# Scalings of the coarse probabilities on ScalarE, one more unit with exps by tiles, and a seventh unit in the first stage of an attention and feed-forward kernel

## The chip, the core and the metric

The kernel runs on one core of a Trainium2 chip. The metric is the device time of that core in microseconds (us), the median of several executions. The engines are called PE (TensorE), DVE (VectorE), ACT (ScalarE), POOL (GpSimd) and SP (SyncE, which issues the DMAs here). PEld is PE's load of the stationary operand.

## What is computed

```python
# q, k, v: (4, 8, 576, 64)
def sm_attn(qq, kk, vv):
    s = scale * np.matmul(qq, kk.transpose(0, 1, 3, 2))
    ...
    return np.matmul(a, vv)          # a = softmax(s)
q_d = q.reshape(B, H, Sd, 4, D).mean(axis=3)     # k_d, v_d the same; Sd = 144
out_up = np.repeat(sm_attn(q_d, k_d, v_d), 4, axis=2)
mask = np.abs(pos[:, None] - pos[None, :]) < 4
scores = np.where(mask, scale * q k^T, -1e9)
out_local = softmax(scores) @ v
x = (out_up + out_local) as (2304, 512)          # rows: batch and position, columns: head and dim
h = x @ w_in                                     # (2304, 2048)
out = (h * np.tanh(log1p(np.exp(np.minimum(h, 20.0))))) @ w_out
```

So there is a coarse attention over positions averaged by fours, a local attention over a band of 7 positions, and a feed-forward part over the sum of both.

## The kernel before

**Units.** Attention is cut into 16 units, one for each batch b (0 to 3) and each pair of heads p (0 to 3). Counted in order, unit 4b+p is (b, p). A unit runs in `attention()` (line 332): the load of `qk` (L350) and sums by fours on DVE (L351, `qkd`); the coarse scores `sc` on PE (L366), their maximum on DVE (L369, L371), three exps with sums on ACT (L373, `A`), the reciprocal (L376, L378), and the scaling of the probabilities. The scaling has two forms: for the units in the list `AMUL` three activations of 128x128 on ACT (L381), for the others one DVE instruction over 128x384 (L384). A small rest, `Ar`, is scaled by DVE in either form (L387). The local scores `sl` (L400, L405) are exponentiated in one of two forms too. For the units in `AEXP` that is nine activations with their own sums, one for each tile of 38 columns (L415, each followed by a read of the accumulator), after a maximum and a small product on DVE (L411, L413). For the others it is a maximum and a subtraction on DVE (L422, L423), one exp over 128x342 on ACT (L425) and a sum on DVE (L426). DVE then scales `L` (L428 to L430). `vv` is loaded (L435) and POOL makes the averaged values (L438, L440, `vd`). PE transposes (L449, L450, L477, L483), ACT copies out of PSUM, PE makes the products with the values (L464, L468, L492), and DVE and ACT add both parts and split them into two words, written into the tiles `x` (L505, L517, L519).

**Slots.** The feed-forward part is 96 slots in `slot()` (line 566): chunk c (0 to 5) of 384 rows against block f (0 to 15) of 128 hidden columns. A slot has twelve matmuls into `h` (L579), five ACT and three DVE instructions (L593 to L605, ending in `g`) and nine matmuls into three accumulators `acc` (L618). Chunks 0 and 1 are interleaved in slots 0 to 31; then come chunks 2 to 5, sixteen slots each. The weights of block f are loaded by SP (L549) into three staging buffers in turn and rebuilt from 64-bit words by ACT and DVE in `load_w()` (L551 to L561).

**Order.** Every operation is recorded with an engine, a planned duration, the buffers it reads and writes, and a priority (lower goes first). `Plan.order()` (line 147) then lays out the order of every engine beforehand: at each step an engine that is free takes the ready operation of lowest priority. The chip executes each engine's list strictly in that order, SP's too. The priorities are: of unit (b, p), `ATT[b][0] + ATT[b][1]*p + UNIT[(b, p)]`, with `VOFF` added for its load of `vv`; of the weights of block f, `WPRI[0] + WPRI[1]*f`, with `WPRI[2]` more for `wo` and `WDMA` more for the load itself; of a slot's `h` about its number s, of its elementwise chain s + 0.2, of its `acc` s + LAG - 0.5, with one LAG for slots under 20, one for 20 to 59 and one from 60.

**Stages.** The first `NPRO` units belong to the first stage (line 661 on). They take turns on four sets of SBUF buffers, `att0`, `att1`, `att2`, `att`, and may use seven PSUM buffers (`props` 4, `attps` 3). The units behind them use the set `att` and the three buffers of `attps` alone, each buffer in the order of the units. When every operation of the first stage is planned to be done (`gate`, line 672, and `done`, line 697), `props` and the sets `att0` to `att2` are closed, and the PSUM of the slots and the weight buffers of blocks 5 to 15 open. The accumulators of chunk 1 lie in `attps` (line 610), so that units 8 and later cannot use it before slot 31 has ended. While PE has nothing to do in the plan, matmuls of constants are put in (`warm`, L705).

Of the kernel before, what the change touches and what calls it, by code (L numbers as in the profile page):

```python
# [19 lines left out]
P = 128  # L20
BIG = 1e30
CH = 384
LAG = (3.0, 4.0, 4.0)
FA = 5
SETS = 3
ATT = {0: (-900, 20), 1: (-46, 10.0), 2: (-4, 16.5), 3: (46, 4.0)}
WPRI = (9.565474018610834, 2.2, 7.7)
UNIT = {(0, 0): -1, (0, 1): -3, (0, 2): -2, (0, 3): -3, (1, 0): 7, (1, 1): -1, (1, 3): 1, (2, 0): 1, (2, 1): -1, (2, 2): 5, (2, 3): 1, (3, 0): 2, (3, 1): 2, (3, 2): 1, (3, 3): -2, (1, 2): -7}
WARM = True
NPRO = 6  # L30
STICK = 15
VOFF = 20
WDMA = 6
PIPE0 = (1, 0, 1)
PIPE1 = (1, 0, 1)
LEAD = 1
PMASK = (0, 1)
AMUL = ((0, 2), (1, 0), (1, 2))
AEXP = ((0, 1), (0, 3))
NMISH = (3, 2)  # L40
TAIL = 0
TICK, BUSY, PACE = 3413.3, 3060, 1.6
# [36 lines left out]
class Plan:  # L79
# [6 lines left out]
    def buf(self, group, tag, shape, dtype=F32, bufs=1, name=None):  # L86
        return Buf(self, group, tag, shape, dtype, bufs, name or f"{tag}_{len(self.ops)}")

    def op(self, eng, dur, fn, r=(), w=(), prio=None, after=(), cold=None, cols=0, gap=0):
        o = Op()  # L90
        o.eng, o.dur, o.fn, o.cold, o.cols, o.gap = eng, dur, fn, cold or 2 * dur, cols, gap
        o.prio = self.prio if prio is None else prio
        o.deps, o.bufs, o.outs, o.seq, o.raw, o.hold = set(after), [], [], len(self.ops), set(), 0.0
        for items, writes in ((r, False), (w, True)):
            for x in items:
                b, key = x if isinstance(x, tuple) else (x, None)
                write = writes or b.group.endswith("ps")
                if b not in o.bufs:
                    o.bufs.append(b)
                    b.left += 1  # L100
                for k, (wr, rd) in b.marks.items():
                    if key is None or k is None or k == key:
                        o.deps.update(wr)
                        o.raw.update(wr)
                        if write:
                            o.deps.update(rd)
                if write:
                    if key is None:
                        b.marks = {None: ({o}, set())}
                    else:  # L110
                        b.marks[key] = ({o}, set())
                else:
                    b.marks.setdefault(key, (set(), set()))[1].add(o)
        o.deps.discard(o)
        self.ops.append(o)
        return o
# [154 lines left out]
def dve(n, fast=False):  # L271
    return 69 + (0.52 if fast else 1.042) * n


def act(n, psum=False, extra=0):
    return (52 if psum else 94) + 0.833 * n + 93 * extra
# [6 lines left out]
class Kernel:  # L283
# [48 lines left out]
    def attention(self, b, p, sb, ps, padded, loose):  # L332
# [45 lines left out]
        op("dve", 88, lambda: nc.vector.reciprocal(cst()[:, 3], cst()[:, 2]), w=[cst])  # L378
        if (b, p) in AMUL:
            for m in range(3):  # L380
# [28 lines left out]
        wide = lambda i: lst()[:, i, :, None].broadcast_to([P, T, KW])  # L409
        if (b, p) in AEXP:  # L410
            op("dve", dve(T * KW), lambda: nc.vector.tensor_reduce(out=lst()[:, 0], in_=sl3(), op=ALU.max, axis=AX.X),  # L411
# [20 lines left out]

        pv_ = pl.prio + VOFF
        vv, vd = buf("vv", [P, 18, P]), buf("vd", [P, 2, P])
# [99 lines left out]
    def load_w(self, f):  # L534
# [6 lines left out]
        for nm, src in (("wi", wi), ("wo", wo)):  # L541
            pl.prio = prio + (WPRI[2] if nm == "wo" else 0)
            st_ = pl.buf("stg", "stg", [P, 512, 2], I32, self.nstg, f"stg_{nm}{f}")
# [5 lines left out]
            op("sp", P * 4096 / RATE, lambda st_=st_, src=src: nc.sync.dma_start(  # L549
                st_().rearrange("p (c f) w -> p c (f w)", c=4), src), w=[st_], prio=pl.prio + WDMA)  # L550
            op("act", act(512), lambda hf=hf: nc.scalar.activation(hf(), hf(), AF.Copy, scale=2.0 ** -112), w=[h])  # L551
# [14 lines left out]
    def slot(self, s, c, f):  # L566
# [46 lines left out]
        for i in range(3):  # L613
# [7 lines left out]
            gi = [g] if len(parts) == 1 else [(g, 2 * i), (g, 2 * i + 1)]  # L621
            op("pe", 700, mm2, r=[*gi, wo], w=[a_], cols=1536, prio=s + LAG[(s >= 20) + (s >= 60)] - 0.5 + 0.1 * i)
            if not last:
# [11 lines left out]
    def run(self, ctx):  # L635
# [28 lines left out]
        for b in (0, 1):  # L664
            for p in range(self.NPAIR):
                if len(units) == NPRO:
                    break
                units.append((ATT[b][0] + ATT[b][1] * p + UNIT.get((b, p), 0), self.attention(
                    b, p, sets[len(units) % len(sets)], ("props", "attps"),
# [4 lines left out]
        for f in range(self.NF):  # L674
            pl.prio = WPRI[0] + WPRI[1] * f
            self.load_w(f)
# [11 lines left out]
        def units(bs):  # L688
            us = [(ATT[b][0] + ATT[b][1] * p + UNIT.get((b, p), 0), self.attention(b, p, "att", "attps", probs["att"], False))
                  for b in bs for p in range(self.NPAIR) if 4 * b + p >= NPRO]  # L690
            self.record(us, PIPE1)
# [82 lines left out]
```

## Time and profile before

| | us |
|---|---|
| median of 3 runs | 522.82 |
| lowest and highest | 521.39, 525.77 |
| the profiled execution, its own time | 524.82 |
| its span, first to last instruction | 522.7 |
| mean granted TensorE clock, share of full | 0.997 |

The profile is of one execution. Busy time counts an engine from the start to the end of its instructions; successive instructions overlap a little, so the step from one start to the next is shorter than a duration. Rows of a timeline give the start, the time, the engine, the line, what is written from what, a count, and in brackets the idle time ahead and what ended it.

### The profile page before, as it was taken

To read this page: it belongs to the slowest core of one execution; us is meant where nothing else is said; L and a number is where in the kernel's file an instruction comes from. 1 tells how busy PE (TensorE), PEld (TensorE's weight loads), DVE (VectorE), ACT (ScalarE), POOL (GpSimd) and SP (SyncE) were. 2 spreads that over 40 slices of the span, in tenths; PEclk is the share of its full clock that TensorE was granted. 3 is DMA by queue.
4 is the path that set the end of the run, shared out by engine and by line. 5 is a ranking of instruction groups with operands and counts; after the bars stand their busy time and mean duration, and the time that the engine had idled before them with its cause. 6 is when DMAs were issued, how large, how long until landed. Compare 5 with 4: busy or idle time off the path is not lost.

```text
span 522.7 us, 11854 instructions
## 1 busy us (share of the span) xinstructions
PE 504.2 (96%) x4896; PEld 435.1 (83%) x4896; DVE 322.6 (62%) x703; ACT 358.0 (68%) x866; POOL 40.4 (8%) x62
## 2 busy tenths in 40 slices
PE   7879979999999999999999999999999999999997
PEld 4657767899988999888898888889999999999995
DVE  6869989999999633677852885564333333333332
ACT  3668778899898756667666666665666556666663
POOL 6431011000000000010110110110000000000000
PEclk9998999999999999999999999999999999999999
DMA  8774465544544001333300453020001000010001
GB/s 345 294 270 150 141 201 201 162 161 130 193 129 154 1 0 57 112 139 136 126 16 0 139 198 131 9 93 0 1 16 46 0 1 1 0 62 0 1 0 60
DMA packets 11861, 50.66 MB, mean 97 GB/s; under 512 B 1312, under 2 KB 1312, under 8 KB 9760
## 3 DMA queue, kind: packets, MB, share of 16 engines
q1 hardware_dynamic: 11808, 49.91, 26.9%
q8 instruction: 38, 0.62, 0.5%
q14 instruction: 15, 0.12, 0.1%
HBM read 45.19 MB, written 4.72 MB: 95 GB/s over the span
## 4 chain that ended last, share of the span: by engine, by line
PE 59%; DVE 14%; ACT 3%; issue 1%; DVEq 0%
PE acc L618 27%; PE h L579 27%; DVE g L605 1%; PE pve L492 1%; DVE mA L594 1%; DVE stg_wo L554 1%; DVE stg_wi L554 1%; PE pt L477 1%; DVE stg_wi L557 1%; DVE x L505 1%; PE pvo L492 1%; DVE x L519 1%; DVE wi L561 1%; DVE Ar_att L387 1%; DVE stg_wo L557 1%
## 5 line engine op out<-in xcount | busy, mean ns | idle before, releaser
L579 PE MATMUL h<-x,wi 128*128 128x384 f32 x1152 | 220.5, 338 | 1.0 <-DVE mH L600 0.9
L618 PE MATMUL acc<-wo,g 128*128 128x512 f32 x864 | 217.8, 395 | 0.3 <-ACT g L603 0.3
L579 PEld LDWEIGHTS h<-x,wi 128*128 128x128 f32 x1152 | 203.3, 188 | 10.3 <-DVE mH L600 2.7
L618 PEld LDWEIGHTS acc<-wo,g 128*128 128x128 f32 x864 | 159.7, 188 | 30.0 <-ACT g L603 0.8
L605 DVE SCALAR_TENSOR_TENSOR g<-mH,g 128x384 fp32r<-128x384 f32 (+1 forms) x98 | 53.5, 547 | 92.9 <-ACT g L603 92.8
L593 ACT ACTIVATE mA<-h 128x384 f32<-128x384 f32 (+1 forms) x98 | 46.8, 480 | 58.6 <-PE h L579 58.1
L596 ACT ACTIVATE mA<-mA 128x384 f32<-128x384 f32 (+1 forms) x98 | 50.5, 517 | 39.7 <-DVE mA L594 39.0
L594 DVE TENSOR_SCALAR mA<-mA 128x384 f32<-128x384 f32 (+1 forms) x98 | 38.7, 396 | 52.7 <-ACT mA L593 52.7
L600 DVE SCALAR_TENSOR_TENSOR mH<-mA,h 128x384 f32<-128x384 f32 (+1 forms) x98 | 52.7, 539 | 18.9 <-ACT mA L599 18.8
L597 ACT ACTIVATE mA<-mA,one 128x384 f32<-128x384 f32 (+1 forms) x98 | 59.5, 608 | 2.4
L603 ACT ACTIVATE g<-mH 128x384 fp32r<-128x384 f32 (+1 forms) x98 | 50.0, 512 | 4.5 <-PE acc L618 2.6
L599 ACT ACTIVATE mA<-mA 128x384 f32<-128x384 f32 (+1 forms) x98 | 49.7, 508 | 0.8
L438 POOL TENSOR_TENSOR vv<-vv 128x512 f32<-128x512 f32 x16 | 21.7, 1358 | 303.5 <-DMA vv<-in_vv_dram 285.1
L373 ACT ACTIVATE A<-sc,cst 128x144 f32<-128x144 f32 x48 | 17.8, 375 | 15.3 <-DVE cst L371 9.2
L517 ACT ACTIVATE x<-x 128x384 fp32r<-128x384 f32 (+1 forms) x32 | 12.4, 434 | 19.8 <-DVE x L505 19.7
L351 DVE TENSOR_REDUCE qkd<-qk 128x288 f32<-128x1152 f32 x16 | 21.5, 1346 | 5.7 <-DMA qk<-in_qk_dram 5.7
L492 PEld LDWEIGHTS pve<-PT,vv 38*64 38x64 f32 x640 | 20.4, 134 | 4.7 <-ACT PT L484 2.6
L492 PE MATMUL pve<-PT,vv 38*64 38x32 f32 x640 | 22.5, 220 | 0.0
L492 PE MATMUL pvo<-PT,vv 38*64 38x32 f32 x512 | 18.3, 221 | 1.8 <-issue 1.6
L705 PE MATMUL warm<-ident 128*128 128x512 bf16 x61 | 17.3, 408 | 1.6 <-POOL ident masks.py:199 1.6
L492 PEld LDWEIGHTS pvo<-PT,vv 38*64 38x64 f32 x512 | 16.4, 133 | 2.0 <-issue 1.7
L366 PE MATMUL sc<-qkd 64*64 64x144 f32 x192 | 16.7, 300 | 0.1
(82 smaller groups left out, 445.1 us busy)
## 6 DMA issues: line engine op xcount, KB each, us to landing
vv<-in_vv_dram SPq DMA_DIRECT2D x16, 1152.0 KB, 6.0
qk<-in_qk_dram SPq DMA_DIRECT2D x16, 582.0 KB, 5.9
stg_wi<-in_w_in_dram SPq DMA_DIRECT2D x16, 512.0 KB, 3.5
stg_wo<-in_w_out_dram SPq DMA_DIRECT2D x16, 512.0 KB, 3.9
out_dram<-o SPq DMA_DIRECT2D x18, 256.0 KB, 2.1
```

Source lines behind the costliest of these rows:

```text
L438: op("pool", gps(512), lambda: nc.gpsimd.tensor_tensor(out=vc()[:, :, 0:2], in0=vc()[:, :, 0:2], in1=vc()[:, :, 2:4], op=ALU.add), w=[(vv, ...
L492: nc.tensor.matmul(o_()[64 * h:64 * h + 64, c0:c0 + 32], vw()[64 * e:64 * e + KW, t // 2, f, 64 * h:64 * h + 64], PT()[64 * e:64 * e + KW, ...
L579: nc.tensor.matmul(h()[:, :CH], w()[:, a, kt * P:(kt + 1) * P], x()[:, b_, :], start=kt == 0 and j == 0, stop=kt == 3 and j == 2)
L593: op("act", act(n, True), lambda o_=o_: nc.scalar.activation(A()[:, o_], h()[:, o_], AF.Exp), r=[h_], w=[a_])
L594: op("dve", dve(n, True), lambda o_=o_: nc.vector.tensor_scalar(A()[:, o_], A()[:, o_], float(math.exp(20.0)), 1.0, op0=ALU.min, op1=ALU.a ...
L596: op("act", act(n), lambda o_=o_: nc.scalar.activation(A()[:, o_], A()[:, o_], AF.Square), w=[a_])
L597: op("act", act(n, False, 1), lambda o_=o_: nc.scalar.activation(A()[:, o_], A()[:, o_], AF.Ln, bias=self.one), w=[a_])
L599: op("act", act(n), lambda o_=o_: nc.scalar.activation(A()[:, o_], A()[:, o_], AF.Exp, scale=-1.0), w=[a_])
L600: op("dve", dve(n), lambda o_=o_: nc.vector.scalar_tensor_tensor(out=H()[:, o_], in0=A()[:, o_], scalar=0.5, in1=h()[:, o_], op0=ALU.subtr ...
L603: op("act", act(n), lambda o_=o_: nc.scalar.activation(g()[:, 0, o_], H()[:, o_], AF.Copy, scale=-2.0), r=[x_], w=[one])
L605: op("dve", dve(n), lambda o_=o_: nc.vector.scalar_tensor_tensor(out=g()[:, 1, o_], in0=H()[:, o_], scalar=-2.0, in1=g()[:, 0, o_].bitcast ...
L618: nc.tensor.matmul(a_(), g()[:, a, i * P:(i + 1) * P], wo()[:, b_], start=first and j == 0, stop=last and j == 2)
```

## The change

Only constants change; the functions stay as they are.

- `AMUL` has all eight units of b = 0 and 1 in place of (0, 2), (1, 0), (1, 2): five more units scale on ACT by three instructions (L381) and not on DVE by one (L384).
- `AEXP` has (1, 1) as well: its local exps go by nine tiles (L411 to L415) and not by L422 to L426.
- `NPRO` is 7 in place of 6: unit 6, (1, 2), joins the first stage. It uses the set `att2` and all seven PSUM buffers, and the gate waits for it. Unit 7, (1, 3), is then the only one behind it on `att` until unit 8.
- Priorities: `VOFF` 40 in place of 20 and `WDMA` 10 in place of 6 (loads of `vv` and of weights later), the step of the weights 2.58 in place of 2.2, LAG 3.5 and 6.0 in place of 3.0 and 4.0 for slots under 20 and from 20 to 59, and new places of the units: (0, 0) at -903, was -901; (1, 0) at -36, was -39; b = 2 at about -4.6, 7.0, 26.6, 36.2, was -3, 11.5, 34, 46.5; b = 3 at about -10.6, 1.7, 19.0, 31.3, was 48, 52, 55, 56.

```diff
-LAG = (3.0, 4.0, 4.0)
+LAG = (3.5, 6.0, 4.0)
-ATT = {0: (-900, 20), 1: (-46, 10.0), 2: (-4, 16.5), 3: (46, 4.0)}
-WPRI = (9.565474018610834, 2.2, 7.7)
-UNIT = {(0, 0): -1, (0, 1): -3, (0, 2): -2, (0, 3): -3, (1, 0): 7, (1, 1): -1, (1, 3): 1, (2, 0): 1, (2, 1): -1, (2, 2): 5, (2, 3): 1, (3, 0): 2, (3, 1): 2, (3, 2): 1, (3, 3): -2, (1, 2): -7}
+ATT = {0: (-900, 20), 1: (-46, 10.0), 2: (-5.642684844573687, 13.604260058964448), 3: (-12.599534886270362, 15.294421654670417)}
+WPRI = (9.565474018610834, 2.5796502663643848, 7.7)
+UNIT = {(0, 0): -3, (0, 1): -3, (0, 2): -2, (0, 3): -3, (1, 0): 10, (1, 1): -1, (1, 3): 1, (2, 0): 1, (2, 1): -1, (2, 2): 5, (2, 3): 1, (3, 0): 2, (3, 1): -1, (3, 2): 1, (3, 3): -2, (1, 2): -7}
-NPRO = 6
+NPRO = 7
-VOFF = 20
-WDMA = 6
+VOFF = 40
+WDMA = 10
-AMUL = ((0, 2), (1, 0), (1, 2))
-AEXP = ((0, 1), (0, 3))
+AMUL = ((0, 0), (0, 1), (0, 2), (0, 3), (1, 0), (1, 1), (1, 2), (1, 3))
+AEXP = ((0, 1), (0, 3), (1, 1))
```

## Rows read from the trace of the kernel before

**Rows 1.** The page's first line.
```profile
span 522.7 us, 11854 instructions
```

**Rows 2.** Busy time by stretch: the stretch, its length, then for PE, PEld, DVE, ACT and POOL the busy us and the number of instructions, the granted clock as a share of full speed, the DMA share and GB/s.
```profile
0.00:31.00 31.00, 25.99 (x566) 15.88 (x566) 22.49 (x54) 16.75 (x73) 14.92 (x38) 1.00 0.79 308
31.00:71.00 40.00, 36.27 (x866) 27.95 (x866) 35.62 (x91) 29.67 (x108) 5.96 (x6) 0.96 0.54 194
71.00:102.88 31.88, 29.10 (x214) 24.52 (x215) 28.41 (x55) 25.54 (x53) 4.62 (x4) 1.00 0.53 179
102.88:211.04 108.16, 107.47 (x539) 96.94 (x538) 81.93 (x164) 88.79 (x175) 0.00 (x0) 1.00 0.31 100
211.04:353.69 142.65, 140.22 (x1889) 120.92 (x1889) 97.03 (x216) 94.27 (x252) 14.92 (x14) 1.00 0.28 100
```

**Rows 3.** The chain of work that ended last, in order of time: start, us, what. Two pieces of one slot, and the last piece of the chain.
```profile
357.85 2.10 PE h L579 x12
359.95 2.08 PE acc L618 x9
...
510.68 8.22 PE acc L618 x36
```

**Rows 4.** Busy time of line 579 alone (the `h` matmuls) in one stretch: PE, PEld, clock, DMA.
```profile
211.04:353.69 142.65, 55.91 (x289) 50.43 (x289) 1.00 0.28 100
```

**Rows 5.** Timeline of PE around unit 8, the first of the units that run between slots (its L492 matmuls left out).
```profile
215.16 0.95 PE L366 MATMUL sc<-qkd 64*64 64x144 f32 x12
...
216.82 2.35 PE L579 MATMUL h<-x,wi 128*128 128x384 f32 x12
...
221.09 0.49 PE L449 MATMUL at<-ident,A 128*128 128x128 f32 x3
...
221.44 2.35 PE L579 MATMUL h<-x,wi 128*128 128x384 f32 x12
223.72 0.47 PE L464 MATMUL pvo<-AT,vd 128*64 128x144 f32 x4
...
224.91 1.63 PE L618 MATMUL acc<-wo,g 128*128 128x512 f32 x6
```

**Rows 6.** Timeline of PE in the first 103 us: the first of a unit's L492 matmuls and what follows them, the first `h` of all, the first product with `vd` of unit 7, and the `h` of the ninth slot (slot 8).
```profile
43.77 0.25 PE L492 MATMUL pve<-PT,vv 38*64 38x32 f32 x2
...
45.05 0.66 PE L477 MATMUL pt<-ident,L_att 128*128 128x128 f32 x4
...
61.70 1.32 PE L579 MATMUL h<-x,wi 128*128 128x384 f32 x6
...
73.17 0.47 PE L464 MATMUL pvo<-AT,vd 128*64 128x144 f32 x4 [2.21 <-POOL vd L440]
...
102.88 2.27 PE L579 MATMUL h<-x,wi 128*128 128x384 f32 x12
```

**Rows 7.** Timeline of DVE in the first 80 us: scalings of `A` in units 1 and 5 with what follows them, the small product of unit 3's exps by tiles, and three waits; the row at 63.75 ends unit 6.
```profile
13.20 1.37 DVE L384 TENSOR_TENSOR A<-A,cst 128x384 f32<-128x384 f32 x1
14.50 0.73 DVE L387 TENSOR_TENSOR Ar_att<-A,cst 128x48 f32<-128x48 f32 x1
...
28.18 0.17 DVE L413 TENSOR_SCALAR lst<-lst 128x9 f32<-128x9 f32 x1
...
47.53 0.55 DVE L384 TENSOR_TENSOR A<-A,cst 128x384 f32<-128x384 f32 x1
48.00 0.17 DVE L428 TENSOR_SCALAR lst<-lst 128x9 f32<-128x9 f32 x1
...
52.79 0.49 DVE L505 TENSOR_TENSOR x<-pve,xd 128x320 f32<-128x320 f32 x1 [0.76 <-ACT A L381]
...
63.75 0.82 DVE L519 TENSOR_TENSOR x<-x,x 128x192 fp32r<-128x192 f32 x2
...
72.29 1.35 DVE L351 TENSOR_REDUCE qkd<-qk 128x288 f32<-128x1152 f32 x1 [1.10 <-DMA qk<-in_qk_dram]
...
75.86 0.43 DVE L552 TENSOR_SCALAR tmp_wi<-stg_wi 128x512 int32<-128x512 int32 x1 [0.88 <-ACT stg_wi L551]
```

**Rows 8.** Timeline of ACT in the first 46 us: one exp by tiles of unit 1 with its accumulator read and the next instruction; the three scalings of unit 2 and the next; the one exp of a unit that is not done by tiles and the next.
```profile
16.07 0.29 ACT L415 ACTIVATE L_att<-sl,lst 128x38 f32<-128x38 f32 x1
...
16.34 0.22 ACT L456 ACTIVATE R_att<-at 16x96 f32<-16x96 f32 x1
...
28.05 0.97 ACT L381 ACTIVATE A<-A,cst 128x128 f32<-128x128 f32 x3
28.93 0.36 ACT L373 ACTIVATE A<-sc,cst 128x144 f32<-128x144 f32 x1
...
44.92 0.48 ACT L425 ACTIVATE L_att<-L_att 128x342 f32<-128x342 f32 x1
45.30 0.37 ACT L373 ACTIVATE A<-sc,cst 128x144 f32<-128x144 f32 x1
```

**Rows 9.** Timeline of SP's queue: the issue of `vv` of unit 6, of `qk` of unit 7, and of `vv` of unit 7.
```profile
45.21 0.33 SPq L435 DMA_DIRECT2D vv<-in_vv_dram  x1
48.89 0.33 SPq L350 DMA_DIRECT2D qk<-in_qk_dram  x1
...
61.87 0.36 SPq L435 DMA_DIRECT2D vv<-in_vv_dram  x1
```

**Rows 10.** Timeline of POOL: the first sum of unit 1's values.
```profile
12.89 1.27 POOL L438 TENSOR_TENSOR vv<-vv 128x512 f32<-128x512 f32 x1 [2.00 <-DMA vv<-in_vv_dram]
```

## The prediction, made before the changed kernel was run

> **What bounds the kernel now.** I read the busy time by stretch first, then the chain of work that ended last, then the timelines of the first 103 us engine by engine. The span is 522.7 us [rows 1], 2.1 us under this execution's own 524.82.
>
> The chain shows the steady state: a slot is 2.10 us of `h` and 2.08 us of `acc` on PE, 4.18 us together, with nothing between [rows 3]. From 102.88 us, the start of slot 8 [rows 6], to 211.04 lie 26 slots; 26 x 4.18 = 108.7, and the stretch took 108.2 [rows 2]. So there PE sets the pace and nothing can be won. The same holds for the last stretch, from 353.69 to the end.
>
> In the stretch 211.04 to 353.69 PE does 24 slots (289 `h` matmuls, twelve a slot [rows 4]) and the eight units of b = 2 and 3. The slots are worth 24 x 4.18 = 100.3 us, so the units cost 142.65 - 100.3 = 42.3 us. A unit's work on PE, by steps from start to start, is 1.66 for both scores, 0.35 for the transposes of `A`, 1.19 for the products with `vd` and the transposes of `L` [rows 5] and 1.28 for L492 [rows 6]: 4.5 us, 36 us for eight. **At most 6.3 us of this stretch is loss.**
>
> Before 102.88 us PE has eight units (36 us), eight `h` and six `acc` (29.3 us): 65 of 103 us. The rest is start-up, constants and waiting. Here PE follows the others. DVE is busy 22.5 of the first 31 us, 35.6 of the next 40 and 28.4 of the 31.9 behind; ACT 16.8, 29.7 and 25.5 [rows 2]. **From 31 to 103 us DVE is the engine nearest to its limit, at 89%**, ACT is at 74 and 80%. What shortens this part moves the whole stream of slots forward, one for one.
>
> **The change part by part.** *Scalings on ACT.* Five units lose L384. Undisturbed it takes 0.47 us of DVE from start to start (47.53 to 48.00), in unit 1 it took 1.30 [rows 7]. Each gains three activations on ACT, 28.05 to 28.93, 0.88 us [rows 8]. *Exps by tiles of (1, 1).* DVE loses L423 and L426, 342 columns each; by the ratio to L384's 384 columns 0.42 us each, and gains L413, 0.17 at most [rows 7]: about 0.7 saved. ACT gains nine exps at 0.27 (16.07 to 16.34) and loses one of 0.38 (44.92 to 45.30): 2.05 us [rows 8].
>
> Units 0, 1 and 3 lie in the first 31 us, units 5 and 7 behind. So behind 31 us DVE saves 2 x 0.47 + 0.7 = 1.6 us, and ACT takes on 2 x 0.88 + 2.05 = 3.8. In 31 to 71 us that would make DVE 34.0 and ACT 33.5 of 40: level. I count the 1.6 as won, between 0 (ACT becomes the pace) and 1.6. In the first 31 us DVE saves 0.47 + 1.30 + 0.47 = 2.2 and ACT takes on 2.6. DVE has 8.5 us idle there and ACT 14.2, so I take 0 from there; it is covered by that idle time. Without that cover the ends are a gain of 2.2 and a loss of 2.6.
>
> L384 of unit 1 took 1.37 us while POOL's L438 ran from 12.89 to 14.16 [rows 7, 10]. The Trainium skill, SBUF — State Buffer, Who interferes with whom, says that a DVE instruction with two inputs in SBUF contends with a GpSimd instruction that reads SBUF, and that ScalarE waits for nobody. The trace agrees; by that rule the moved scaling would also win back the 0.8 us of this stretch, unless the next DVE instruction with two inputs meets L438 in its place.
>
> *The seventh unit.* Unit 6 had begun long before the first `h`: its `vv` was issued at 45.21 and it ended at 64.6, the first `h` being at 61.70 [rows 6, 7, 9]. What is new is its place. On `att` it followed unit 3, and unit 7 followed it: unit 7's `qk` went out at 48.89 and its `vv` only at 61.87, once unit 6 had freed the tile [rows 9]. That is why PE waited 2.21 us for `vd` at 73.17 [rows 6]. On `att2` unit 6 follows unit 2, and unit 7 follows unit 3, whose tiles are free by 45 us. Everything behind a late load in an in-order queue moves with it: in SP's queue the weights stood behind these two loads; in DVE's queue the reduction of unit 8's `qk` at 72.29 stood 1.10 us (it needs unit 7's tile) with slot 0's last instruction and the weights behind it, and 0.88 us was lost at 75.86 for a weight whose load was late [rows 7]. Of these 1.98 us, with 0.76 us at 52.79 that was queued behind a unit-6 instruction, I count **2.2 us** as won, between 0 and 2.7. The lower place of `vv` (VOFF 40) puts `qk` of the next unit ahead of it, the lower place of weights (WDMA 10) the loads of the last units ahead of those. Both cost nothing while the loads come before their use; POOL's two sums of unit 7 follow the earlier load. With that cover gone, a late `vd` costs what it cost at 73.17, 2.2 us.
>
> *The gate* now waits for unit 6. If unit 6 ended at 64.6 as before, the first `h` would be 2.9 us later. I take 0: until then DVE has unit 7 and the weights of the first five blocks, which need no gate, and the early `h` of slots 0 and 1 were not what was late; the elementwise chain behind them was, on DVE. The bound is 2.9.
>
> *The second half.* LAG 6 lets PE take `h` further ahead of `acc`, so that a late `g` stops it less; units of b = 3 are no longer held back to slots 48 on. Both act on the 6.3 us of loss and on nothing else. No row shows a run with another LAG. I take a quarter, 1.6 us: most of the loss is inside the units' own chains on a single set of buffers, which stays single. The ends are 5 won, and 4 lost if units packed closer hold up the slots' chain on ACT and DVE. LAG 3.5 and the step of the weights only shift what DVE does first among work that must all be done by 103 us: 0.
>
> **Sum:** -1.6 - 2.2 - 1.6 = **-5.4 us**. Against this execution's own time that is 524.82 - 5.4 = 519.4; the execution is 2.0 above the median, so against the median 522.82 it is **517.4 us**, faster by 1.03%.
>
> **Rivals.** *(a) Hidden.* The start of slot 8 is set by the total of DVE's and ACT's work for units, weights and slots, and the waits that go are filled by waits elsewhere, since ACT gains 3.8 us where it is already at 74%. For it: ACT and DVE come out level. Against it: the waits at 72 to 76 us have one cause, the shared set, and it goes. Then only the second half counts: 522.8 - 1.6, about 521. That the seventh unit changes nothing, because it was already running at 45 us, is this case too.
>
> *(b) ScalarE becomes the bound.* All 6.4 us of new ACT work (5 x 0.88 + 2.05) lands on the path of the first stage: in the first 31 us unit 1 has its nine exps already and gets its scaling as well, and from 31 to 71 us ACT goes from 29.7 to 33.5 of 40. It decides once ACT's idle time there cannot be used because each idle piece is a wait for PE or DVE in the chain of one unit. Then 522.8 + 6.4 = **529**, slower. Against it: in 31 to 71 us 10.3 us of ACT are free and several units are in flight. The Trainium skill, ScalarE: Activation LUTs, Rules for kernel authors, puts multiplications on VectorE rather than ScalarE, and so speaks for this rival; the rows agree about the price, 0.88 against 0.47 us a unit, but not about which engine has room.
>
> *(c) All waits go.* The start gains 1.6 + 2.7 + 2.2, the second half 5: 522.8 - 11.5 = 511.3.
>
> **Chances.** The forecast (513.5 to 520.5) 0.46; hidden 0.24; ScalarE 0.13; all waits go 0.17. About 1% (5.2 us, so 517.6 and 528.0) is what a measurement of this kernel can tell from no change. Faster by over 1%: 0.17 and 0.28 of the forecast's 0.46, together 0.45. Within 1%: 0.18 and 0.24, together 0.42. Slower: 0.13. A range from 511.5 to 525.5 leaves out (b) and less than half of (c), under 2 in 10.
>
> **What would show it.** Right: `vv` of unit 7 is issued well before 61.87, PE does not wait for `vd` near 73, slot 8's `h` starts about 99 us (102.88 less 3.8) and stretch 211 to 354 is about 1.6 us shorter for its 24 slots and eight units. DVE's busy time falls by about 4 us and ACT's grows by about 6.4. Wrong: slot 8 at 103 us or later with ACT above 90% from 31 to 71 us is (b); an unchanged start with the waits gone elsewhere is (a); a first `h` later than 64 us with DVE idle ahead of it means that the gate costs what I took as nothing.

## The result, and the profile after

The changed kernel takes **529.96 us** (528.68 to 533.33, 4 runs) against 522.91 before: ratio **1.0121**, 95% interval 1.0081 to 1.0161. Timed again beside the kernel before (run e5) it is 527.54 against 523.52, 1.0069 (1.0041 to 1.0096). It is slower where I had forecast faster by 1%. The ratios leave out the executions marked as slow on record (one of 988 us, the profiled one of e8, one of 822 us in e13, one of 528.7 us in e9 and four of the kernel before); the medians count all.

The profiled execution took 533.33 us, the longest of the first four. Its busy time by stretch answers to [rows 2]; the columns are the same.

```profile
0.00:31.00 31.00, 26.57 (x576) 16.35 (x576) 20.64 (x51) 20.13 (x89) 14.41 (x38) 1.00 0.89 347
31.00:71.00 40.00, 34.78 (x797) 24.51 (x798) 30.88 (x75) 26.86 (x112) 8.18 (x8) 0.81 0.38 146
71.00:102.88 31.88, 31.34 (x248) 26.55 (x247) 29.12 (x57) 27.05 (x55) 2.42 (x2) 0.97 0.49 170
102.88:211.04 108.16, 108.00 (x546) 97.42 (x545) 85.12 (x170) 90.34 (x179) 0.00 (x0) 1.00 0.31 103
211.04:353.69 142.65, 136.93 (x1868) 116.83 (x1867) 97.94 (x216) 93.48 (x248) 15.37 (x14) 1.00 0.30 106
```

Two things differ. From 31 to 71 us the granted clock is 0.81 (before 0.96), and DVE and ACT are *less* busy than before, 30.9 and 26.9 us. ACT waits for PE there (10.5 us, of them 8.6 for the transposes of `A`, L450); DVE waits 2.9 us for PE and 5.6 for ACT. From 211 to 354 us PE is busy 3.3 us less than before: it stands more.

PE's timeline shows the first, with the rows that answer to [rows 6].

```profile
9.42 2.12 PE L705 MATMUL warm<-ident 128*128 128x512 bf16 x9
...
59.73 0.31 PE L492 MATMUL pve<-PT,vv 38*64 38x32 f32 x1 [1.35 <-issue]
...
69.02 4.05 PE L705 MATMUL warm<-ident 128*128 128x512 bf16 x9
...
73.56 0.77 PE L579 MATMUL h<-x,wi 128*128 128x384 f32 x3
74.25 0.47 PE L464 MATMUL pvo<-AT,vd 128*64 128x144 f32 x4
...
106.89 1.40 PE L579 MATMUL h<-x,wi 128*128 128x384 f32 x7
```

PE stood 1.35 us, from 58.38 to 59.73, for nothing that the profile shows. Towards the end of this stand the clock fell to half (1.2 GHz): its share is 1.00 from 58 to 59 us, 0.77 in the next microsecond and 0.50 in the one after. Nine constants then took 4.05 us where nine took 2.12 at full clock. The first `h` came at 73.56 (before 61.70), slot 8 at 106.89 (before 102.88). But the wait for `vd` of [rows 6] is gone at 74.25. SP's queue shows why; the rows are the issue of unit 8's `qk`, of the first weights and of unit 7's `vv`, which left at 61.87 before [rows 9].

```profile
49.35 0.33 SPq L350 DMA_DIRECT2D qk<-in_qk_dram  x1
49.73 0.43 SPq L549 DMA_DIRECT2D stg_wi<-in_w_in_dram  x1
50.25 0.38 SPq L435 DMA_DIRECT2D vv<-in_vv_dram  x1
```

From the start of slot 8 to the end of the span it takes 531.3 - 106.9 = **424.4 us**; before it was 522.7 - 102.9 = **419.8**. So of 8.6 us in the profiled executions 4.0 arise ahead of slot 8 and **4.6 behind it**. PE's waits from 103 to 360 us (total us, times, longest), first before, then now, are these:

```profile
PE at L450 <- DVE Ar_att L387: 2.1, 4, 0.7
PE h L579 <- DVE mH L600: 0.7, 2, 0.5
PE pvo L464 <- ACT AT L453: 0.3, 1, 0.3
```

```profile
PE pvo L468 <- ACT R_att L456: 2.7, 3, 1.2
PE h L579 <- DVE mH L600: 2.1, 3, 1.1
PE sl L405 <- issue: 0.6, 1, 0.6
PE pve L492 <- ACT PT L484: 0.4, 1, 0.4
```

They sum to 3.1 us before and 5.8 now. Of the 4.6 us these waits show 2.7, and the wait of `h` for L600 is 1.4 of the growth; the rest of the 4.6 is in no wait listed here.

### The profile page after: what moved, and what is told of

It is laid out like the page before. It is cut to its first block, busy times and chain, and to the rows that moved or that the text cites. A ratio compares the mean times of both kernels' runs of the same rounds, so it can differ in the third digit from the quotient of the medians.

```text
span 531.3 us, 11838 instructions
## 1 busy us (share of the span) xinstructions
PE 511.5 (96%) x4892; PEld 437.9 (82%) x4892; DVE 323.7 (61%) x697; ACT 365.3 (69%) x898; POOL 40.4 (8%) x62
## 4 chain that ended last, share of the span: by engine, by line
PE 73%; DVE 15%; ACT 7%; issue 2%; DMA 1%; POOL 1%; DVEq 0%; ACTq 0%; POOLq 0%
PE h L579 32%; PE acc L618 31%; PE pve L492 2%; PE warm L705 2%; PE sc L366 1%; DVE mA L594 1%; DVE x L519 1%; DVE x L505 1%; PE pvo L492 1%; PE sl L405 1%; DVE mH L600 1%; PE pt L477 1%; DVE L_att L430 1%; DVE g L605 1%; ACT A L373 1%
## 5 line engine op out<-in xcount | busy, mean ns | idle before, releaser
L618 PE MATMUL acc<-wo,g 128*128 128x512 f32 x864 | 214.1, 393 | 0.0
L605 DVE SCALAR_TENSOR_TENSOR g<-mH,g 128x384 fp32r<-128x384 f32 (+1 forms) x98 | 55.1, 564 | 88.7 <-ACT g L603 88.6
L594 DVE TENSOR_SCALAR mA<-mA 128x384 f32<-128x384 f32 (+1 forms) x98 | 37.2, 381 | 65.3 <-ACT mA L593 65.0
L600 DVE SCALAR_TENSOR_TENSOR mH<-mA,h 128x384 f32<-128x384 f32 (+1 forms) x98 | 53.1, 542 | 3.1 <-ACT mA L599 1.8
L438 POOL TENSOR_TENSOR vv<-vv 128x512 f32<-128x512 f32 x16 | 21.0, 1313 | 283.1 <-DMA vv<-in_vv_dram 242.4
L492 PEld LDWEIGHTS pve<-PT,vv 38*64 38x64 f32 x640 | 21.8, 142 | 7.9 <-issue 3.8
L492 PE MATMUL pve<-PT,vv 38*64 38x32 f32 x640 | 23.9, 227 | 2.7 <-issue 1.4
L705 PE MATMUL warm<-ident 128*128 128x512 bf16 x66 | 22.1, 474 | 1.6 <-POOL ident masks.py:199 1.6
L492 PE MATMUL pvo<-PT,vv 38*64 38x32 f32 x512 | 19.4, 227 | 0.3 <-ACT xd L472 0.2
L705 PEld LDWEIGHTS <-ident 128*128 128x128 bf16 x100 | 9.1, 110 | 11.6 <-issue 6.9
```

What stands on the lines that cost most here:

```text
L492: nc.tensor.matmul(o_()[64 * h:64 * h + 64, c0:c0 + 32], vw()[64 * e:64 * e + KW, t // 2, f, 64 * h:64 * h + 64], PT()[64 * e:64 * e + KW, ...
L594: op("dve", dve(n, True), lambda o_=o_: nc.vector.tensor_scalar(A()[:, o_], A()[:, o_], float(math.exp(20.0)), 1.0, op0=ALU.min, op1=ALU.a ...
L600: op("dve", dve(n), lambda o_=o_: nc.vector.scalar_tensor_tensor(out=H()[:, o_], in0=A()[:, o_], scalar=0.5, in1=h()[:, o_], op0=ALU.subtr ...
L605: op("dve", dve(n), lambda o_=o_: nc.vector.scalar_tensor_tensor(out=g()[:, 1, o_], in0=H()[:, o_], scalar=-2.0, in1=g()[:, 0, o_].bitcast ...
L618: nc.tensor.matmul(a_(), g()[:, a, i * P:(i + 1) * P], wo()[:, b_], start=first and j == 0, stop=last and j == 2)
L705: nc.tensor.matmul(t, ib[:, :P], ib[:, None].broadcast_to([P, 2, 256])[:, :max(1, n // 256), :min(n, 256)], start=first, stop=first)
```

## The experiments

The table has the median, the ratio to the kernel before on the same chip with its interval (the figure on record, not the quotient of two medians, from which it differs by up to 0.004), and from the one profiled execution the start of slot 8's `h`, the time at half clock ahead of it (worked out from the granted clock), the time from slot 8 to the end of the span, and PE's waits of `h` for L600 from 103 to 360 us.

| run | median us | ratio (95%) | slot 8 at | half clock | slot 8 to end | waits for L600 |
|---|---|---|---|---|---|---|
| before | 522.91 | 1 | 102.9 | 3.4 | 419.8 | 0.7 |
| changed kernel | 529.96 | 1.0121 (1.0081 to 1.0161) | 106.9 | 17.1 | 424.4 | 2.1 |
| e5, the same again | 527.54 | 1.0069 (1.0041 to 1.0096) | 102.8 | 10.2 | 424.7 | 2.6 |
| e1, LAG and late units back | 523.19 | 0.9975 (0.9937 to 1.0013) | 100.2 | 6.8 | 419.8 | none |
| e9, the same again | 522.59 | 0.9960 (0.9929 to 0.9992) | 103.1 | 6.8 | 420.6 | 0.4 |
| e2, LAG 4 alone back | 525.71 | 1.0012 (0.9970 to 1.0054) | 100.6 | 3.4 | 421.2 | 0.4 |
| e3, late units alone back | 526.09 | 1.0037 (0.9994 to 1.0079) | 99.3 | 3.4 | 424.6 | 3.3 |
| e13, before with LAG 6 | 529.91 | 1.0090 (1.0053 to 1.0127) | 102.6 | 6.8 | 421.2 | 1.5 |
| e7, LAG 5 | 530.89 (1 run) | | 105.3 | 17.1 | 423.7 | 0.3 |
| e6, a third `g` | 528.81 | 1.0078 (1.0047 to 1.0108) | 102.9 | 10.2 | 423.9 | 1.1 |
| e14, a third `mH` | 525.68 (1 run) | | 100.8 | 3.4 | 422.8 | 0.4 |
| e4, six units | 531.50 | 1.0136 (1.0066 to 1.0206) | 105.7 | 6.8 | 421.8 | none |
| e8, e1 with six units | 530.46 | 1.0102 (1.0064 to 1.0139) | | | | |
| e11, e1 with scalings back | 525.13 | 1.0043 (1.0012 to 1.0075) | 101.9 | 0 | 420.1 | 0.2 |
| e12, e1 with loads back | 525.87 | 1.0023 (0.9993 to 1.0054) | 105.3 | 3.4 | 420.9 | none |
| e10, e1 with more constants | 523.56 | 0.9984 (0.9955 to 1.0014) | 101.1 | 3.4 | 420.9 | 0.2 |
| e15, before with seven units | 524.83 | 1.0024 (0.9995 to 1.0052) | 101.4 | 0 | 422.0 | 1.3 |
| e16, before with scalings and exps | 531.71 | 1.0154 (1.0109 to 1.0200) | 113.4 | 17.1 | 419.6 | 0.5 |

### Behind slot 8: LAG or the units' places (e1, e2, e3, e13)

e1 puts back LAG for slots 20 to 59 and the places of the units of b = 2 and 3; e2 the LAG alone, e3 the places alone. PE's order up to about slot 20 stays that of the changed kernel.

```diff
-LAG = (3.5, 6.0, 4.0)
+LAG = (3.5, 4.0, 4.0)                       # e1, e2
-ATT = {..., 2: (-5.64..., 13.60...), 3: (-12.59..., 15.29...)}
+ATT = {..., 2: (-4, 16.5), 3: (46, 4.0)}    # e1, e3; UNIT[3, 1] = 2
```

> The changed kernel with LAG 4.0 for slots 20 to 59 and the places of the units of b = 2 and 3 as before; the order of every engine up to about slot 20 stays that of the changed kernel. Theory A (the change loses in two places: about 4.3 us where the units of b = 2 and 3 run between slots, the rest in the first 103 us): 529.96 - 4.3 = 525.7, and from the start of slot 8's h to the end of the span about 4.5 us less than in the changed kernel. Theory B (all is lost in the first 103 us and only carried on): 530, no difference behind slot 8.

> The changed kernel with LAG 4.0 for slots 20 to 59 alone; the units of b = 2 and 3 keep their earlier places. If the larger LAG makes the loss behind slot 8 (its h run in pairs, and h then waits for the DVE instruction that frees its PSUM): 525.7, as with both back. If the closer packing of the units makes it: 530.

> The changed kernel with the places of the units of b = 2 and 3 as before, LAG stays 6.0. If the closer packing makes the loss behind slot 8: 525.7. If the larger LAG makes it: 530. If each makes half: about 528 here and in the run with LAG 4.0 alone.

e1 measured 419.8 us behind slot 8, as before, and 0.9975. So theory A holds: the loss behind slot 8 belongs to these two edits, and theory B falls. Of the two the LAG is the larger: with LAG 6.0 alone left it is 424.6 (e3), with the places alone left 421.2 (e2). These are single executions. By the times both may count, 0.0062 and 0.0037 above e1 (3.2 and 1.9 us), but the intervals overlap, so the times do not show which is larger; e3's median, 526.09 (beside 524.24 for the kernel before on that chip), is even near the 525.7 that was written for the closer packing as the cause.

PE's waits of e3 from 103 to 360 us, then those of e1:

```profile
PE h L579 <- DVE mH L600: 3.3, 3, 1.4
PE at L450 <- DVE Ar_att L387: 0.9, 1, 0.9
PE acc L618 <- issue: 0.8, 1, 0.8
```
```profile
PE at L450 <- DVE Ar_att L387: 1.8, 3, 1.0
PE pvo L464 <- ACT AT L453: 0.2, 1, 0.2
```

The reader is to see that the wait for L600, the instruction that frees the PSUM of `h`, is 3.3 us with LAG 6.0 and not listed with 4.0. It is not tied to LAG 6.0 alone: with 4.0 it is 0.7 us in the kernel before and 1.3 in e15.

e13 sets LAG 6.0 in the kernel before and nothing else.

```diff
-LAG = (3.0, 4.0, 4.0)
+LAG = (3.0, 6.0, 4.0)
```

> The kernel before with LAG 6.0 in place of 4.0 for slots 20 to 59 and nothing else; every order up to about slot 20 is that of before. If LAG 6.0 costs by itself: PE waits 2 us or more for the DVE instruction that frees h (L600) between 103 and 360 us, from slot 8 to the end 423.5 to 424.7 in place of 419.8, ratio to the kernel before 1.008. If it costs only together with the changed first stage (with six units there and LAG 6.0 it was 421.8): 420 to 421.5, ratio 1.000 to 1.003.

1.0090: LAG 6.0 costs by itself, 4.7 us, as written for that case. The trace does not bear out the rest of it: behind slot 8 it took 421.2 us, which was written for the rival, with 1.5 us of the waits for L600.

```profile
PE h L579 <- DVE mH L600: 1.5, 3, 0.8
```

The profiled execution was the quickest of its runs (525.55, the others 526.94 to 531.40). Where those lost the rest no trace shows.

### What PE waits for with LAG 6 (e6, e7, e14)

```diff
-NMISH = (3, 2)
+NMISH = (2, 2)   # e6: mA 2, and g with 3 buffers
+NMISH = (2, 3)   # e14: mA 2, mH 3, g 2
-LAG = (3.5, 6.0, 4.0)
+LAG = (3.5, 5.0, 4.0)   # e7 alone
```

> The changed kernel, LAG 6.0, with three buffers of g in place of two, and two of mA in place of three to make room (with two of mA alone the order of no engine changes). Theory C (with LAG 6.0 the slots in flight fill h, mH and g, two buffers each; then every acc must end before the next g, the next mH and the next h, and an attention instruction queued on ACT or DVE in that loop stops PE): with seven buffers LAG 6.0 no longer fills them, and from slot 8 to the end it takes 419.8 to 421.2 in place of 424.4. Theory D (LAG 6.0 costs by the order of acc itself, whatever the buffers): 424 again.

> The changed kernel with LAG 5.0 in place of 6.0 for slots 20 to 59. Theory C: a slot less in flight than the six buffers hold, so most of the loss behind slot 8 is gone: 421 to 422 from slot 8 to the end. Theory D: in proportion, about 422.8, half way between 421.2 at LAG 4.0 and 424.4 at 6.0.

> The changed kernel, LAG 6.0, with three buffers of mH in place of two (and two of mA, which alone changes no order). If L600 comes late because it waits for a free mH, which comes from g, which comes from an acc: the waits of PE's h on L600 fall from 2.1 to 3.3 us to under 1 between 103 and 360 us, and the stretch from slot 8 to the end goes under 423. If L600 comes late because of what is queued ahead of it on ACT and DVE, the units' instructions above all: 2 us or more of these waits, 424.

PE's waits from 103 to 360 us in e14, then in e6:

```profile
PE at L450 <- DVE Ar_att L387: 2.7, 3, 1.1
PE sl L405 <- issue: 0.5, 1, 0.5
PE h L579 <- DVE mH L600: 0.4, 1, 0.4
```
```profile
PE at L450 <- DVE Ar_att L387: 2.7, 3, 1.1
PE h L579 <- DVE mH L600: 1.1, 2, 0.9
```

With a third `mH` the wait for L600 falls to 0.4 us, with a third `g` to 1.1, with LAG 5.0 to 0.3: in this part theory C holds, the wait is one for the loop of buffers. But the stretch behind slot 8 was won back only by 1.6 us, 0.5 and 0.7, in one execution each: in all three plans PE waits 2.7 to 3.4 us for `Ar` (L387), which the changed kernel did not (the kernel before, 2.1). As forecasts of this stretch, theory C's numbers failed for e6 (423.9) and e7 (423.7), e14's came (422.8). Theory D's number came for e6 (424) and not for e7 (422.8). So for the stretch as a whole D is not ruled out, and e6 won no time (1.0078 against e5's 1.0069 on the same chip). Each new plan puts L387 elsewhere in DVE's queue, and I did not find an edit that keeps it in place.

### The first stage: the changed kernel again, and six units (e5, e4, e8)

> The changed kernel once more, unaltered, timed beside the others on one chip. Its profile of the first time had 17 us at half clock between 45 and 73 us. If that belongs to the order of this kernel (theory: its queue holds PE below full clock every time), slot 8 again starts near 106 and the time is 530. If it is chance (the runs with the same first stage and LAG 4.0 had slot 8 at 99.3 to 100.6), slot 8 starts near 100 and the time is near 525 to 527; the 4.6 us behind slot 8 stay in either case (424.4 from slot 8 to the end).

Slot 8 started at 102.8 with 10.2 us at half clock and the median was 527.54, so neither theory's numbers were met. The same order of PE up to slot 8 gave these starts in e3, e1, e5:

```profile
99.26 2.26 PE L579 MATMUL h<-x,wi 128*128 128x384 f32 x12
```
```profile
100.25 2.26 PE L579 MATMUL h<-x,wi 128*128 128x384 f32 x12
```
```profile
102.78 2.26 PE L579 MATMUL h<-x,wi 128*128 128x384 f32 x12
```

Over seven executions of this order it is 99.3 and 100.6 with 3.4 us at half clock, 100.2 and 103.1 with 6.8, 102.8 with 10.2, 105.3 and 106.9 with 17.1: slot 8 comes later the longer the time at half clock, under one and the same order. That the clock makes the difference, and not something that delays both, is likely but not shown by itself. The 424.7 us behind slot 8 stayed, as both said.

e4 and e8 have `NPRO = 6`, e4 in the changed kernel, e8 in e1.

> The changed kernel with six units in the first stage. Theory A1 (packing seven units into the first stage starves PE of instructions, it stands, its clock halves and the constants in its queue are then in the way of real work): less than 7 us at half clock before 103 us, slot 8 starts 3 us or more sooner than 106.9, about 526 to 527. Theory A2 (ScalarE's extra work is the bound of the first stage, whatever the number of units): slot 8 at about 106, 529 to 530. That the gate waits for unit 6 is tested too: with six units the first h should start near 62 to 66 in place of 73.6.

> LAG 4.0 and the places of b = 2 and 3 as before, with the first stage of the changed kernel but for six units in place of seven. If the seventh unit is what brings slot 8 forward from 102.9 to about 100: slot 8 at 103 to 106, time 526 to 529. If it is the scalings and exps on ScalarE: slot 8 near 100 to 101, time as with seven units, 523.

e8 is slower than with seven units by 0.0142 against e9, 7.4 us, and slower than both of its numbers; it has no usable trace. e4 is not clear of the changed kernel (1.0136 against 1.0121 and 1.0069). A1 falls as far as it blames the seventh unit: half clock was down to 6.8 us, as written, but slot 8 came only 1.2 us sooner and the time did not fall. A2's place of slot 8 came (105.7), yet ACT was busy 30.7 us of the 40 from 31 to 71 us, no more than in e1 (32.0), where slot 8 came at 100.2; PE stood 3.8 us there for L600 before 103 us. So given the other edits, the seventh unit is needed. The first `h` did come early with six units (63.7), and slot 8 still at 105.7. So the first `h` is not what sets slot 8.

### The first stage: its other parts (e9 to e12)

e9 is e1 timed again; e10 is e1 with PACE 2.6 (was 1.6); e11 is e1 with `AMUL` and `AEXP` as before; e12 is e1 with `VOFF = 20` and `WDMA = 6`.

> LAG 4.0 and the places of b = 2 and 3 as before, the first stage of the changed kernel, timed in five rounds. The forecast of the first stage (3.8 us won there, less what half clock takes back) gives 0.993 of the kernel before; the first timing gave 0.9975 (0.9937 to 1.0013). Theory A: clear of no change, 0.993 to 0.997. Rival (what the first stage wins is lost again to time at half clock): 0.998 to 1.001.

> The same with PACE 2.6 in place of 1.6: 83 constant matmuls of 512 columns are planned for PE in place of 66; every order changes with it. If PE's half clock between 57 and 73 us is what moves slot 8 (it started at 99.3 to 100.6 with none or 3.4 us of it there, 102.8 with 6.8, 105.3 and 106.9 with 13.7), and more constants prevent it: no half clock behind 50 us, slot 8 before 100, 519 to 521. If the constants are in the way of real work: slot 8 at 101 or later with the clock full.

> As the run with LAG 4.0 and the old places of b = 2 and 3, but with the scalings and the exps of (1, 1) back on DVE (AMUL and AEXP as before), still seven units in the first stage. If moving 3.8 us off DVE brings slot 8 forward as forecast (1.6 us): slot 8 at 101.5 to 102.5, time 1.6 us longer. If ScalarE's extra work costs as much as DVE's saves: no difference, slot 8 at 100. If ScalarE is the bound: slot 8 before 99.

> As the run with LAG 4.0 and the old places of b = 2 and 3, but with VOFF 20 and WDMA 6 as before. If the later places of the loads bring unit 2 forward (its sc at 14.3 in place of 20.3) and with it slot 8: unit 2's sc near 20 and slot 8 at 101 to 103. If they cost, by putting unit 8's qk and unit 7's vv ahead of the weights (first weights issued at 49.7 in place of 28.3): slot 8 before 99. If nothing hangs on them: 100.

e9: 0.9960, just clear of 1: the first stage of the change wins 2.1 us (1.1 by the medians), and this is the quickest version of the study. Its own profiled execution, 3.1 us above its median, does not show the gain (slot 8 at 103.1); those of e1, e2 and e3 do. With more constants (e10) the half clock behind 50 us was gone, 3.4 us ahead of it stayed, and slot 8 came at 101.1 with no gain in time: that is what was written for constants in the way of real work. Taking the scalings back costs 0.0083 against e9 (4.3 us, 2.5 by the medians), taking the places of the loads back 0.0063 (3.3 us), with unit 2's `sc` at 24 and slot 8 at 105.3. The step of the weights, LAG 3.5 and the places of units 0 and 4 were not tried apart from the rest.

### One part alone on the kernel before (e15, e16)

> The kernel before with seven units in the first stage and nothing else. If the seventh unit wins by itself what the first stage as a whole wins (2 us): slot 8 at 100 to 101, ratio 0.996. If it wins only with the places of the loads and the scalings that go with it (taking either back cost 3 to 4 us): slot 8 at 103 to 106, ratio 1.000 to 1.006.

> The kernel before with all scalings of units 0 to 7 on ACT and the exps of (1, 1) by tiles, and nothing else. If the 3.8 us taken off DVE shorten the first stage by themselves: slot 8 at 99 to 101.5, ratio 0.993 to 0.997. If they do so only with the seventh unit: 103, 1.000; if ScalarE becomes the bound: slot 8 at 104 or later.

Alone, the seventh unit does not help (1.0024, not clear of 1): in its trace slot 8 came 1.5 us sooner, at 101.4, and the part behind it took 2.2 us longer. The scalings and exps on ACT alone cost 8 us (1.0154): slot 8 at 113.4, 17.1 us at half clock. That is past the 104 written for ScalarE as the bound, but ACT was busy only 32.3 us of the 40 from 31 to 71 us; what delayed slot 8 here is open. Parts that each cost 3 to 7 us when taken out win nothing or cost 8 us when put in alone.

## Why the prediction was wrong

*The second half: -1.6 forecast, +4.6 measured (424.4 and 424.7 against 419.8).* This is the step that failed. It read: "LAG 6 lets PE take `h` further ahead of `acc`, so that a late `g` stops it less". The page of the kernel before has the row that speaks against it, and I did not weigh it; the last numbers are the idle time ahead of all `acc` matmuls and what ended it.

```profile
L618 PE MATMUL acc<-wo,g 128*128 128x512 f32 x864 | 217.8, 395 | 0.3 <-ACT g L603 0.3
```

A late `g` stopped PE for 0.3 us in the whole span, and not once from 103 to 360 us. Of the "at most 6.3 us" of loss the listed waits there show 3.1, and none is of this kind: a larger LAG had next to nothing to win. And it had a price. PE runs ahead until the buffers of `h`, `mH` and `g` are full; from then on the next `h` needs an L600, that a free `mH`, that an `acc` just done. A unit's instruction queued in that loop then stops PE. This is how I read the waits for L600; in the changed kernel DVE shows it at 240 us:

```profile
240.68 1.27 DVE L428 TENSOR_SCALAR lst<-lst 128x9 f32<-128x9 f32 x1
241.85 0.54 DVE L605 SCALAR_TENSOR_TENSOR g<-mH,g 128x384 fp32r<-128x384 f32 x1
242.32 0.20 DVE L429 RECIPROCAL lst<-lst 128x9 f32<-128x9 f32 x1
242.45 0.54 DVE L600 SCALAR_TENSOR_TENSOR mH<-mA,h 128x384 f32<-128x384 f32 x1
```
```profile
243.04 1.83 PE L579 MATMUL h<-x,wi 128*128 128x384 f32 x9 [0.87 <-DVE mH L600]
```

L428 of a unit took 1.27 us, L605 and L600 stood behind it, and the next `h` came 0.87 us late. L428 took 0.17 us in [rows 7]; here it ran from 240.68 beside POOL's L438 (240.40 to 241.90), as L384 did in [rows 7, 10]. That the LAG costs is shown by e13, where it is the only edit, and e2 and e3 fit it; that the wait for L600 is one for `mH` too is shown by e14. But this wait is only 1.4 of the 4.6 us; the other waits of this stretch, for L456 (2.7 us) and L387, move with every plan, and which of them the change caused is open. My bound for this term, 4 lost, fell just short of its size; the value that I took had the wrong sign.

*The first stage: -3.8 forecast, -2.1 measured (e9).* The sign was right, and slot 8 was forecast at 99: it started at 99.3 in the quickest of seven starts, with 3.4 us at half clock, so this agreement is partly luck. What failed is the sum by terms. Scalings (1.6 forecast) are worth 2.5 to 4.3 when taken out, the seventh unit (2.2) 7.4, the loads (0) 3.3, while alone the scalings lose 8 and the seventh unit wins nothing. I priced each edit against an order that stands still, but the planner lays out all five queues anew for each; that is my reading of why the prices do not add up.

*The waits.* `vv` of unit 7 left 11.6 us earlier and PE's wait for `vd` at 73 us went, as forecast. *The gate.* I took 0 with a bound of 2.9. The first `h` came 3.8 to 11.9 us later, past the bound and past the 64 us that was to show a cost; that this in itself costs nothing is in line with e4, and with e3, where the first `h` came at 65.5 and slot 8 at 99.3. *ScalarE.* It was not the bound: 26.9 us of 40 from 31 to 71 us in the profile after, 32.0 in e3, far from the 90% that was to show rival (b). That (b)'s 529 is close to the measured 529.96 is luck. ACT's busy time over the span grew by 7.3 us to 365.3 (forecast 6.4). DVE's did not fall by 4 in this execution, 323.7 after 322.6; it did in e1, 318.2.

*What I left out.* The time at half clock. No rival had it, though [rows 2] show 0.96 from 31 to 71 us before. It goes with the gap between 1.0121 and 1.0069: the granted clocks of the first four executions give 10.3 us at half clock on average, those of e5 6.3. How much of that gap it makes is open.

## What to carry to other kernels

Before a queue is allowed to run further ahead, read the idle time ahead of the instruction that it is meant to help: at 0.3 us there is next to nothing to win, and a lead as long as all the buffers of the chain can turn a delay in the chain into a wait. In a kernel whose order comes from a planner, as here, an edit's price need not be its instructions' time; two runs with the edit alone and with all but the edit say more than a sum. Compare the same order over several executions before explaining a few microseconds in a stage that runs partly at half clock.

## What the runs showed of the hardware

In the changed kernel PE stands for 1.35 to 1.75 us at a time with nothing to wait for in the profile, in stretches of many small matmuls, as at 59.73 us above; before 103 us it has three such waits over 1 us, 4.5 us in all, the kernel before one (1.6 us).

```profile
PE at L449 <- issue: 1.7, 1, 1.7
PE warm L705 <- POOL ident masks.py:199: 1.6, 1, 1.6
PE sc L366 <- issue: 1.4, 1, 1.4
PE pve L492 <- issue: 1.4, 1, 1.4
```

These are PE's longest waits in the first 103 us of the changed kernel. What the engine lacked then no run here shows. With two of the three stands the granted clock fell to half: with the one that ended at 45.38 us half a microsecond later, with the one that ended at 59.73 just ahead of its end. With the longest, 1.75 us, which ended at 36.61, it did not fall. In e11 it did not fall before 103 us at all, with these waits:

```profile
PE sl L405 <- issue: 2.6, 2, 1.7
PE pvo L492 <- issue: 2.0, 1, 2.0
PE pve L492 <- issue: 1.8, 1, 1.8
```

So a stand of this length alone does not bring the clock down. Once it had fallen in the changed kernel, the constants planned for keeping it up took twice their time in front of the units' own matmuls.
